# Attention head output copied whole, its halves crossed by transfers, a small add on another engine, and weight loads at other steps

## The chip, the core and the metric

The kernel runs on one core of one Trainium2 chip. The metric is the device time of one execution in microseconds (us), here the median of three timed runs. One further execution was profiled, and all rows below come from it. The engines are named as the profile names them: PE is TensorE (PEld is its weight load), DVE is VectorE, ACT is ScalarE, POOL is GpSimd, SP is SyncE, and SPq is the queue from which SP issues transfers.

## What is computed

Sixteen attention heads (batch 2, heads 8) over 768 rows of 64 values. A hash of six bits per row decides which keys a query may see. Two feed-forward layers follow, on 1536 tokens of 512 values with 2048 hidden values each.

```python
q_bucket = sum(((q @ proj) > 0) * 2 ** arange(6))          # the same for k
mask = q_bucket[..., :, None] == k_bucket[..., None, :]
scores = where(mask, (q @ k.T) / sqrt(64), -1e9)
scores = scores - max(scores)
attn = exp(scores)
attn = attn / (sum(attn) + 1e-09)
x = concat_heads(attn @ v)                                 # 1536 x 512
h = x @ moe_w_in;   x = (h * sigmoid(1.702 * h)) @ moe_w_out
h = x @ moe2_w_in;  out = (h * tanh(softplus(h))) @ moe2_w_out
```

## The kernel before, in words

Products are made in a rounded 32-bit form, and each operand is split into a high part and a low remainder, so that a product is two or three matmuls. The mask is a product too: each operand of the score product holds 32 rows of scaled bits (the mask rows) beside the remainder rows, and masked scores come out very large.

Attention is one loop over 96 steps, six for each head n (a step is one block of 128 queries against 768 keys). The source is written in the order in which each engine executes, and nothing is reordered. The letters of `ORDER = "ACaBbETQPR"` give the order within step i:

- A and B (`trp`): PE transposes two 128-key tiles of the three exponentiated blocks finished three steps earlier or less, and ACT copies each to its rounded high part (L421). a and b (`trl`): DVE subtracts to get the low part (L426).
- C (`clamp`): DVE clamps the scores and finds their minimum (L368). E (`expo`): ACT takes the exponential and sums each row into one column of `z` (L379).
- T: everything that was booked for this step by `at(step, function)`. Q (`qk`): the four score matmuls of the next step (L355), of which the last two read the mask rows.
- P and R (`pv`): four matmuls with the values (L438, L439). Three steps make one half (384 queries) of a head's weighted sum, in one PSUM tile `u`. After the sixth product of a half, `u_out` empties it.

Booked functions around the change, with step numbers for head n:

- `norm0` (L391, L392) at 6(n+1)+3: add 1e-9 to the row sums and take the reciprocal. `norm1` and `norm2` at 6(n+1)+5: transpose them on PE (L396), copy them out of PSUM (L402) and store them to DRAM (L403). `norm3` two steps later reads them back, broadcast to 64 partitions (`rb`, L409).
- `u_out` runs at the end of every third step, and for the second half of head n at 6(n+1)+3. Head pairs share tiles: `uh` takes each head's main half-sum at its own 64 partitions, `ul` takes the other 64 partitions crossed over. Both are ACT copies of 64x384 (L455, L456). The PSUM tile exists once, so the next half's first product waits for the second copy.
- `x_out` (POOL, L462, L463) adds `uh` and `ul` and multiplies by `rb`, at 12(u+1)+11 for pair u, and `x_split` (POOL) six steps later writes the tokens' high and low parts. For the last pair both run inside the feed-forward part.
- `start_prep` at 6(n-2)+2: POOL scales and splits q and k of head n (L251 to L258), with a transfer `qx<-qk_m` (L252). One head later, PE makes the hash bits (L266), DVE compares them (`mk`, L280), and at 6n-3 four transfers carry the mask rows to their operands (`qb<-mk`, `kb<-mk`, L292, L293). They are needed by the score matmuls of step 6n, which are issued at step 6n-1.
- Weights: `wfetch` starts 512 KB loads (`raw`, L103), three buffers in all. Five of them are converted inside attention (`wgo`: L112 and L126 on ACT, L114, L116, L118 on DVE, L128 on POOL), one in every second head from about step 31. Their loads are booked at st-15 and at st+6, where st is 32, 44, 56, 68 and 80.

All transfers are issued by SP in program order, and an issue that waits holds up those behind it. The feed-forward part `moe` follows; it issues one 12-matmul product after another on PE, while ACT and DVE convert weights, activate and split.

Of the kernel before, what the change touches and what calls it, by code (L numbers as in the profile page):

```python
# [10 lines left out]
F32 = mybir.dt.float32  # L11
# [3 lines left out]
ALU = mybir.AluOpType  # L15
# [21 lines left out]
def lsh_attention_moe_kernel(  # L37
# [10 lines left out]
    nc = tc.nc  # L48
    B, H, D, S = qt.shape
    NTOK, DM = out.shape  # L50
    P = 128
    NT = S // P
# [3 lines left out]
    HS = S // 2  # L56
# [4 lines left out]
    NPRE = 5  # L61
# [102 lines left out]
    def attention():  # L164
        with ExitStack() as es:
# [4 lines left out]
            sm = es.enter_context(tc.tile_pool(name="sm", bufs=12))  # L170
            ptp = es.enter_context(tc.tile_pool(name="ptp", bufs=4))
            uo = es_u.enter_context(tc.tile_pool(name="uo", bufs=2, side="right"))
# [168 lines left out]
            pt_t = {}  # L341
            u_t = {}
            xs_t = {}
            z_t = {}
            rb_t = {}
            scr = dr.tile([NHD, S], F32, name="scr")

            def qk(i):
                n, t = divmod(i, NT)
                kh, qx, qb, kb, _ = opnd[n]  # L350
                s = ps_s.tile([P, 2, 512], F32, tag="s", name="s")
                c = slice(t * P, (t + 1) * P)
                for a, bb, st in ((qx, kh, True), (qb, kb, False)):
                    for f in range(2):
                        nc.tensor.matmul(  # L355
                            s[:, f, :HS],
                            a[:, c],
                            bb[:, f * HS : (f + 1) * HS],
                            start=st,
                            stop=not st,  # L360
                        )
                st_t[i] = s
# [10 lines left out]
            def expo(i):  # L373
                sb, mn = st_t.pop(i)
                n, t = divmod(i, NT)
                p = sb.rearrange("p a b -> p (a b)")
                if t == 0:
                    z_t[n] = sm.tile([P, NT], F32, tag="z", name="z", bufs=2)
                nc.scalar.activation(  # L379
                    p,  # L380
                    p,
                    AF.Exp,
                    bias=mn,
                    scale=-1.0,
                    accum_out=z_t[n][:, t : t + 1],
                )
                p_t[i] = p

            def norm0(n):
                z = z_t[n]  # L390
                nc.vector.tensor_scalar(z, z, 1e-9, None, ALU.add)  # L391
                nc.vector.reciprocal(z, z)  # L392

            def norm1(n):
                pt = ps_t.tile([P, 512], F32, tag="pt", name="prep")
# [3 lines left out]
            def norm2(n):  # L399
                pt = z_t.pop(n)  # L400
                zt = sm.tile([NT, P], F32, tag="zt", name="zt", bufs=1)
                nc.vector.tensor_copy(zt, pt[:NT, :P])  # L402
                nc.sync.dma_start(scr[n].rearrange("(t p) -> t p", p=P), zt)  # L403

            def norm3(n):
# [25 lines left out]
            def pv(g, t):  # L431
                n, f = divmod(g, 2)
                hi, lo, _ = pt_t.pop((g, t))
                if t == 0:
                    u_t[g] = ps_u.tile([P, 512], F32, tag="u", name="u")
                ut = u_t[g]
                vv = opnd[n][4][0]
                nc.tensor.matmul(ut[:, :HS], vv[:, t, :], hi, start=(t == 0), stop=False)  # L438
                nc.tensor.matmul(ut[:, :HS], vv[:, t, :], lo, start=False, stop=(t == NT - 1))  # L439
                if t == NT - 1:  # L440
                    u_out(g)

            def u_out(g):
                n, f = divmod(g, 2)
                u, h = divmod(n, 2)
                ut = u_t.pop(g)
                if h == 0 and f == 0:
                    uh = uo.tile([P, S], F32, tag="uh", name="uh")
                    ul = uo.tile([P, S], F32, tag="ul", name="ul")
                    xs_t[u] = (uh, ul)  # L450
                uh, ul = xs_t[u]
                c = slice(f * HS, (f + 1) * HS)
                here = slice(h * D, (h + 1) * D)
                there = slice((1 - h) * D, (2 - h) * D)
                nc.scalar.copy(uh[here, c], ut[here, :HS])  # L455
                nc.scalar.copy(ul[here, c], ut[there, :HS])  # L456

            def x_out(u):
                uh, ul = xs_t.pop(u)
                rb = rb_t.pop(u)  # L460
                xs_t[u] = ul
                nc.gpsimd.tensor_add(ul, ul, uh)  # L462
                nc.gpsimd.tensor_mul(ul, ul, rb)  # L463

# [17 lines left out]
            second[2]()  # L482
            LAG = 3
            ORDER = "ACaBbETQPR"
            PVLAG = LAG + 1
            todo = {}

            def at(step, f, *args):
                todo.setdefault(step, []).append((f, args))

            def prep_at(n):
                return 5 if n == 2 else NT * (n - 2) + 2
# [14 lines left out]
            for u in range(NHD // 2 - 1):  # L507
                at(2 * NT * (u + 1) + XO, x_out, u)
                at(2 * NT * (u + 1) + XO + NT, x_split, u)
            for n in range(NHD):  # L510
                if n > 1:
                    at(prep_at(n), start_prep, n)
                if n >= 2:
                    at((0, 6)[n - 2] if n < 4 else NT * (n - 3) + 2, load_q, n)
                    at((0, 6)[n - 2] if n < 4 else NT * (n - 3) + 2, load_k, n)
                if n >= 2 and n % 2 == 0:
                    at(max(8, NT * (n - 2) + 1), load_v, n // 2)
                at(NT * (n + 1) + 3, norm0, n)
                at(NT * (n + 1) + 5, norm1, n)
                at(NT * (n + 1) + 5, norm2, n)  # L520
                at(NT * (n + 1) + 7, norm3, n)

            for k in range(NPRE):
                st = NSTEP - 4 - 2 * NT * (NPRE - k)
                at(st - 15, wfetch, k + 1)
                for off in (-1, 0, 2, 5, 8, 9):
                    at(st + off, wgo, k, 1, nc.gpsimd.tensor_sub)
                at(st + 6, wfetch, k + 4)
            at(NSTEP, load_table, SET_GELU)

            qk(0)
            for i in range(NSTEP + PVLAG):
                if i == NSTEP:
# [6 lines left out]
                g, j = divmod(kk, 3)  # L540
                kv = i - PVLAG
                gv, jv = divmod(kv, 3)
                for op in ORDER:
                    if op == "A" and tr:
                        trp(g, 2 * j)
                    elif op == "B" and tr:
                        trp(g, 2 * j + 1)
                    elif op == "a" and tr:
                        trl(g, 2 * j)
                    elif op == "b" and tr:  # L550
                        trl(g, 2 * j + 1)
                    elif op == "C" and i < NSTEP:
                        clamp(i)
                    elif op == "E" and i < NSTEP:
                        expo(i)
                    elif op == "Q" and i + 1 < NSTEP:
                        qk(i + 1)
                    elif op == "P" and 0 <= kv < NSTEP:
                        pv(gv, 2 * jv)
                    elif op == "R" and 0 <= kv < NSTEP:  # L560
                        pv(gv, 2 * jv + 1)
                    elif op == "T":
                        while todo and min(todo) <= i:
                            st = min(todo)
                            f, args = todo[st].pop(0)
                            if not todo[st]:
                                del todo[st]
                            f(*args)
                for part in range(max(0, 2 * (i - NSTEP)), min(2 * (i - NSTEP) + 2, 2 * KD)):
                    gemm_in(part // KD, part % KD, part % KD + 1)  # L570
            for st in sorted(todo):
                for f, args in todo[st]:
                    f(*args)
            late.append(lambda: x_out(NHD // 2 - 1))
            late.append(lambda: x_split(NHD // 2 - 1))

    def moe():
        with ExitStack() as es:
# [69 lines left out]
            for i in range(2, N + OLAG):  # L648
# [36 lines left out]
                gemm_out(i - OLAG)  # L685

    attention()
    moe()

# [56 lines left out]
```

## Time and profile before

| | us |
|---|---|
| median of three runs | 783.54 |
| lowest, highest | 782.67, 786.53 |
| the profiled execution | 783.52 |
| its span, first to last instruction | 781.5 |
| PE busy in the span | 758.0 |
| DVE, ACT, POOL busy | 434.6, 397.6, 184.4 |

The attention loop takes about the first 250 us and the two feed-forward layers the rest. [...] Busy time of PE is the union of pipelined matmuls with modelled ends, so a matmul that had to wait a little for its input still leaves a short tail that counts as busy.

### The profile page before, as it was taken

The page shows a single profiled execution, that of the slowest core. Times are in us where ns is not written, and L with a number is a line of the kernel's source. Part 1 is how long each engine was busy: PE and PEld are TensorE (multiplying, and loading weights), DVE is VectorE, ACT ScalarE, POOL GpSimd, SP SyncE. Part 2 cuts the span into 40 slices and gives each one's busy share as a digit, 9 for nine tenths or more (in the row PEclk, how much of TensorE's full clock was granted, in tenths as well). Part 3 has the DMA queues.
Part 4 walks back from the last instruction along what each step waited for, and adds up shares of the span by engine and source line. Part 5 has one row for each costly group of instructions (what it writes and reads, how often), then busy time and mean ns, then how long its engine had stood idle before and what let it go on. Part 6 is the DMA issues. An engine that isn't in the chain of part 4 may idle for free.

```text
span 781.5 us, 10532 instructions
## 1 busy us (share of the span) xinstructions
PE 758.0 (97%) x3760; PEld 642.4 (82%) x3760; DVE 434.6 (56%) x823; ACT 397.6 (51%) x796; POOL 184.4 (24%) x173
## 2 busy tenths in 40 slices
PE   5999999999999999999999999999999999999998
PEld 4999887888888788888888888888888888888886
DVE  6888889889897799941111677869311211121111
ACT  5888887888888466641212555466221212222121
POOL 7857867869633400000000000000000000000000
PEclk9999999999999999999999999999999999999999
DMA  5475574354420255610000144435000100010001
GB/s 164 131 177 129 134 201 133 88 150 122 114 74 20 68 202 199 201 69 1 0 1 1 64 152 162 135 96 174 0 1 1 54 1 1 0 55 1 0 1 54
DMA packets 23971, 65.04 MB, mean 83 GB/s; under 512 B 4048, under 2 KB 6192, under 8 KB 23920
## 3 DMA queue, kind: packets, MB, share of 16 engines
q1 hardware_dynamic: 23920, 64.39, 27.9%
q8 instruction: 29, 0.48, 0.3%
q14 instruction: 22, 0.18, 0.1%
HBM read 49.38 MB, written 3.19 MB: 67 GB/s over the span
## 4 chain that ended last, share of the span: by engine, by line
PE 79%; DVE 6%; ACT 5%; DMA 3%; POOL 3%; issue 3%; SPq 1%; DVEq 0%; POOLq 0%; ACTq 0%
PE y L612 33%; PE h L159 32%; PE s L355 4%; PE pt L414 4%; ACT p L379 2%; PE u L438 2%; PE u L439 2%; ACT pth L421 2%; PE prep L266 2%; POOL qx L254 1%; DMA vn<-in_vt_dram 1%; DMA kb<-mk 1%; DVE ptl L426 1%; DVE p L368 1%; DVE z L391 1%
## 5 line engine op out<-in xcount | busy, mean ns | idle before, releaser
L596 DVE TENSOR_TENSOR gl<-h,gh 128x512 fp32r<-128x512 f32 x96 | 66.2, 690 | 267.2 <-ACT h L595 266.8
L594 ACT ACTIVATE gh<-h 128x512 fp32r<-128x512 f32 x96 | 57.3, 597 | 256.1 <-PE h L159 255.5
L159 PE MATMUL h<-x_hi,wl 128*128 128x512 f32 x384 | 149.6, 389 | 0.9 <-DVE wl L128 0.9
L159 PE MATMUL h<-x_hi,wh 128*128 128x512 f32 x384 | 149.5, 389 | 0.0
L159 PE MATMUL h<-x_lo,wh 128*128 128x512 f32 x384 | 149.4, 389 | 0.0
L426 DVE TENSOR_TENSOR ptl<-pt,pth 128x384 fp32r<-128x384 f32 x192 | 97.8, 550 | 30.7 <-ACT pth L421 30.2
L379 ACT ACTIVATE p<-p,mn 128x768 f32<-128x768 f32 x96 | 90.5, 943 | 15.6 <-DVE p L368 15.1
L414 PE MATMUL pt<-ident,p 128*128 128x128 f32 x576 | 85.5, 277 | 8.8 <-DVE ptl L426 4.8
L421 ACT CAST pth<-pt 128x384 fp32r<-128x384 f32 x192 | 82.5, 483 | 22.1 <-PE pt L414 21.4
L368 DVE TENSOR_SCALAR_CACHE_REDUCE p<-s 128x768 f32<-128x768 f32 x96 | 90.2, 940 | 0.9 <-PE s L355 0.8
L159 PEld LDWEIGHTS h<-x_hi,wl 128*128 128x128 f32 x384 | 72.1, 188 | 16.3 <-DVE wl L128 1.3
L414 PEld LDWEIGHTS pt<-ident,p 128*128 128x128 f32 x576 | 66.7, 140 | 22.6 <-DVE ptl L426 9.8
L159 PEld LDWEIGHTS h<-x_hi,wh 128*128 128x128 f32 x384 | 72.1, 188 | 15.0 <-issue 0.2
L159 PEld LDWEIGHTS h<-x_lo,wh 128*128 128x128 f32 x384 | 72.0, 188 | 14.7
L612 PE MATMUL y<-gh,wl 128*128 128x512 f32 x192 | 74.8, 390 | 0.1
L612 PE MATMUL y<-gh,wh 128*128 128x512 f32 x192 | 74.7, 389 | 0.0
L612 PE MATMUL y<-wh,gh 128*128 128x512 f32 x192 | 74.7, 389 | 0.0
L612 PE MATMUL y<-wl,gh 128*128 128x512 f32 x192 | 74.7, 389 | 0.0
L612 PE MATMUL y<-gl,wh 128*128 128x512 f32 x192 | 74.7, 389 | 0.0
L612 PE MATMUL y<-wh,gl 128*128 128x512 f32 x192 | 74.7, 389 | 0.0
L438 PE MATMUL u<-pth,vv 128*128 128x384 f32 x192 | 65.8, 343 | 0.7 <-ACT ul L456 0.7
L439 PE MATMUL u<-ptl,vv 128*128 128x384 f32 x192 | 64.6, 337 | 0.0
(85 smaller groups left out, 1132.2 us busy)
## 6 DMA issues: line engine op xcount, KB each, us to landing
raw<-in_wt_dram SPq DMA_DIRECT2D x64, 512.0 KB, 3.3
kn<-in_kt_dram SPq DMA_DIRECT2D x16, 384.0 KB, 5.9
qn<-in_qt_dram SPq DMA_DIRECT2D x16, 192.0 KB, 4.2
vn<-in_vt_dram SPq DMA_DIRECT2D x8, 384.0 KB, 5.4
rb<-scr SPq DMA_DIRECT2D x16, 192.0 KB, 3.4
out_dram<-ob SPq DMA_DIRECT2D x12, 256.0 KB, 2.0
qx<-qk_m SPq DMA_DIRECT2D x15, 192.0 KB, 5.2
qb<-qk_m SPq DMA_DIRECT2D x15, 192.0 KB, 4.4
```

The source lines that it names most:

```text
L159: nc.tensor.matmul(h, a[:, wk], x[:, kk], start=(n == 0), stop=(n == 3 * KD - 1))
L355: nc.tensor.matmul(s[:, f, :HS], a[:, c], bb[:, f * HS : (f + 1) * HS], start=st, stop=not st,)
L368: nc.vector.tensor_scalar(sb, s[:, :, :HS], NEG, None, ALU.min, ALU.min, accum_out=mn)
L379: nc.scalar.activation(p, p, AF.Exp, bias=mn, scale=-1.0, accum_out=z_t[n][:, t : t + 1],)
L414: nc.tensor.transpose(ptile[:, j * P : (j + 1) * P], p_t[3 * g + j][:, t * P : (t + 1) * P], ident,)
L421: nc.scalar.copy(hi, ptile[:, :HS])
L426: nc.vector.tensor_sub(lo, ptile[:, :HS], rnd(hi))
L438: nc.tensor.matmul(ut[:, :HS], vv[:, t, :], hi, start=(t == 0), stop=False)
L439: nc.tensor.matmul(ut[:, :HS], vv[:, t, :], lo, start=False, stop=(t == NT - 1))
L594: nc.scalar.activation(gh, h, fn)
L596: nc.vector.tensor_sub(gl, h, rnd(gh))
L612: nc.tensor.matmul(y[j], w[:, js] if m == 0 else x[:, js], x if m == 0 else w, start=(first and n == 0), stop=(last and n == 2),)
```

## The change

`u_out` now makes one ACT copy of all 128 partitions of a half, into a tile for each head (`u0` for the first head of a pair, `u1` for the second). When a head is complete, SP transfers do the crossing: for the first head `ul[0:64] <- u0[64:128]`, for the second `ul[64:128] <- u1[0:64]` and `u0[64:128] <- u1[64:128]`, 192 KB each. The add of 1e-9 goes to POOL at step 6(n+1)+1 (the reciprocal stays on DVE at +3), the small copy of `norm2` goes from DVE to ACT, and the first five weight loads are booked at st-10 and three more at steps 76, 82 and 88.

```diff
             def norm0(n):
                 z = z_t[n]
-                nc.vector.tensor_scalar(z, z, 1e-9, None, ALU.add)
-                nc.vector.reciprocal(z, z)
+                nc.gpsimd.tensor_scalar(z, z, 1e-9, 1.0, ALU.add, ALU.mult)
+
+            def norm0b(n):
+                nc.vector.reciprocal(z_t[n], z_t[n])
...
-                nc.vector.tensor_copy(zt, pt[:NT, :P])
+                nc.scalar.copy(zt, pt[:NT, :P])
...
-                if h == 0 and f == 0:
-                    uh = uo.tile([P, S], F32, tag="uh", name="uh")
-                    ul = uo.tile([P, S], F32, tag="ul", name="ul")
-                    xs_t[u] = (uh, ul)
-                uh, ul = xs_t[u]
-                c = slice(f * HS, (f + 1) * HS)
-                here = slice(h * D, (h + 1) * D)
-                there = slice((1 - h) * D, (2 - h) * D)
-                nc.scalar.copy(uh[here, c], ut[here, :HS])
-                nc.scalar.copy(ul[here, c], ut[there, :HS])
+                if f == 0:
+                    uh_t[n] = uo.tile([P, S], F32, tag=f"u{h}", name="uh", bufs=2 - h)
+                uh = uh_t[n]
+                nc.scalar.copy(uh[:, f * HS : (f + 1) * HS], ut[:, :HS])
+                if f == 1 and h == 0:
+                    xs_t[u] = uo.tile([P, S], F32, tag="ul", name="ul")
+                    nc.sync.dma_start(xs_t[u][0:D], uh[D:P])
+                elif f == 1:
+                    nc.sync.dma_start(xs_t[u][D:P], uh[0:D])
+                    nc.sync.dma_start(uh_t[n - 1][D:P], uh[D:P])
...
+                at(NT * (n + 1) + 1, norm0, n)
+                at(NT * (n + 1) + 3, norm0b, n)
...
-                at(NT * (n + 1) + 3, norm0, n)
-                at(NT * (n + 1) + 5, norm1, n)
-                at(NT * (n + 1) + 5, norm2, n)
-                at(NT * (n + 1) + 7, norm3, n)
+                at(NT * (n + 1) + NZ, norm1, n)
+                at(NT * (n + 1) + NZ, norm2, n)
+                at(NT * (n + 1) + NZ + 2, norm3, n)
...
-                at(st - 15, wfetch, k + 1)
+                at(st - 10, wfetch, k + 1)
                 for off in (-1, 0, 2, 5, 8, 9):
                     at(st + off, wgo, k, 1, nc.gpsimd.tensor_sub)
-                at(st + 6, wfetch, k + 4)
+            for j in range(3):
+                at(st - 4 + 6 * j, wfetch, NPRE + 1 + j)
```

NZ is 5, so `norm1` to `norm3` keep their steps.

## Rows read from the trace of the kernel before

**Rows 1.** Windows: length, busy us (count) of each engine, clock, DMA share, GB/s.
```profile
35.00:91.60 56.60, 56.42 (x366) 52.41 (x365) 49.15 (x114) 50.08 (x115) 40.99 (x37) 1.00 0.60 145
91.60:232.30 140.70, 132.70 (x821) 116.60 (x821) 126.12 (x267) 117.49 (x262) 98.91 (x87) 1.00 0.47 126
...
281.50:330.00 48.50, 48.50 (x216) 40.17 (x215) 46.63 (x83) 32.45 (x56) 0.00 (x0) 1.00 0.61 200
```

**Rows 2.** Timeline, first score matmuls of chosen steps on PE: start, us, what.
```profile
35.04 0.60 PE L355 MATMUL s<-kh,qx 128*128 128x384 f32 x2
...
44.85 0.60 PE L355 MATMUL s<-kh,qx 128*128 128x384 f32 x2
46.92 0.59 PE L355 MATMUL s<-kh,qx 128*128 128x384 f32 x2
...
91.63 0.59 PE L355 MATMUL s<-kh,qx 128*128 128x384 f32 x2
...
119.57 0.60 PE L355 MATMUL s<-kh,qx 128*128 128x384 f32 x2
...
123.01 0.60 PE L355 MATMUL s<-kh,qx 128*128 128x384 f32 x2
...
232.32 0.60 PE L355 MATMUL s<-kh,qx 128*128 128x384 f32 x2
```

**Rows 3.** Groups by line on DVE, 91.6 to 232.3: busy us, mean ns, idle before.
```profile
L426 DVE TENSOR_TENSOR ptl<-pt,pth 128x384 fp32r<-128x384 f32 x108 | 55.0, 549 | 14.0 <-ACT pth L421 13.6
...
L391 DVE TENSOR_SCALAR z<-z 128x6 f32<-128x6 f32 x9 | 6.1, 677 | 0.0
...
L402 DVE COPY zt<-prep 6x128 f32<-6x128 f32 x9 | 2.4, 269 | 0.0
```

**Rows 4.** Timeline, DVE's small steps and POOL beside them.
```profile
104.21 0.15 DVE L391 TENSOR_SCALAR z<-z 128x6 f32<-128x6 f32 x1
...
150.74 1.83 POOL L463 TENSOR_TENSOR ul<-ul,rb 128x768 f32<-128x768 f32 x1
...
151.28 1.33 DVE L391 TENSOR_SCALAR z<-z 128x6 f32<-128x6 f32 x1
...
152.53 0.52 POOL L77 TENSOR_SCALAR vv<-vn 128x384 fp32r<-128x384 f32 x1
152.64 0.19 DVE L392 RECIPROCAL z<-z 128x6 f32<-128x6 f32 x1
```

**Rows 5.** Groups by line on ACT, the same stretch.
```profile
L456 ACT COPY ul<-u 64x384 f32<-64x384 f32 x18 | 8.5, 474 | 0.3
```

**Rows 6.** Waits in that stretch: us in total, times, longest.
```profile
POOL wl L128 <- ACT wh L126: 25.7, 4, 6.6
...
PEld s L355 <- DMA kb<-mk: 2.5, 5, 1.4
...
PE s L355 <- DMA kb<-mk: 1.3, 2, 1.1
```

**Rows 7.** Transfers: KB each, us to landing; stretches 58 to 60.7, 196.7 to 199.3, whole.
```profile
kb<-mk SPq DMA_DIRECT2D x2, 48.0 KB, 2.6
...
kb<-mk SPq DMA_DIRECT2D x2, 48.0 KB, 5.2
...
qx<-qk_m SPq DMA_DIRECT2D x15, 192.0 KB, 5.2
```

**Rows 8.** Timeline: the last mask-row transfer of a head, and PE waiting for it.
```profile
136.03 0.59 SPq L293 DMA_DIRECT2D kb<-mk  x1
...
139.35 0.19 PEld L355 LDWEIGHTS s<-kb,qb 128*128 128x128 f32 x1 [0.16 <-DMA kb<-mk]
```

**Rows 9.** Timeline of POOL and DVE where the feed-forward part begins.
```profile
258.91 1.85 POOL L462 TENSOR_TENSOR ul<-ul,uh 128x768 f32<-128x768 f32 x1 [14.44 <-ACT ul L456]
...
264.43 2.13 POOL L463 TENSOR_TENSOR ul<-ul,rb 128x768 f32<-128x768 f32 x1 [3.67 <-DMA rb<-scr]
...
264.77 2.33 DVE L128 TENSOR_TENSOR wl<-wb,wh 128x512 fp32r<-128x512 f32 x1
```

More of the change, by code (lines that the diff above doesn't have):

```diff
@@ L343, in attention @@
             xs_t = {}
+            uh_t = {}
             z_t = {}
@@ L377, in expo @@
                 if t == 0:
-                    z_t[n] = sm.tile([P, NT], F32, tag="z", name="z", bufs=2)
+                    z_t[n] = sm.tile([P, NT], F32, tag="z", name="z", bufs=3)
                 nc.scalar.activation(
@@ L446, in u_out @@
                 ut = u_t.pop(g)
-                if h == 0 and f == 0:
-                    uh = uo.tile([P, S], F32, tag="uh", name="uh")
-                    ul = uo.tile([P, S], F32, tag="ul", name="ul")
-                    xs_t[u] = (uh, ul)
-                uh, ul = xs_t[u]
-                c = slice(f * HS, (f + 1) * HS)
-                here = slice(h * D, (h + 1) * D)
-                there = slice((1 - h) * D, (2 - h) * D)
-                nc.scalar.copy(uh[here, c], ut[here, :HS])
-                nc.scalar.copy(ul[here, c], ut[there, :HS])
+                if f == 0:
[8 more added lines that the diff above has]
+                    nc.sync.dma_start(uh_t[n - 1][D:P], uh[D:P])
             def x_out(u):
-                uh, ul = xs_t.pop(u)
+                ul = xs_t[u]
+                uh = uh_t.pop(2 * u)
                 rb = rb_t.pop(u)
-                xs_t[u] = ul
                 nc.gpsimd.tensor_add(ul, ul, uh)
@@ L484, in attention @@
             ORDER = "ACaBbETQPR"
+            NZ = 5
             PVLAG = LAG + 1
```

## The prediction

> **What bounds the kernel now.** I read the windows first, then the starts of score matmuls, then the groups, waits and transfers of the stretch that stood out. The windows [rows 1] show three regimes. From 281.5 us PE is busy 48.50 of 48.50: the feed-forward part is PE's own work, the change doesn't touch it, and what attention gains moves all of it forward. From 35.0 to 91.6 (heads 2 to 5) PE is busy 56.42 of 56.60, and a head takes 56.59/4 = 14.15 us, from the starts at 35.04 and 91.63 [rows 2]. From 91.63 to 232.32 (heads 6 to 14, with the weight conversions) it is different: nine heads take 140.69 us, 15.63 each; PE is busy 132.7, DVE 126.1 of 140.7 (0.896) and ACT 117.5. A plain step lasts 46.92 - 44.85 = 2.07, but one such as 119.57 to 123.01 lasts 3.44 [rows 2]. No engine is full there; DVE is nearest to it for the work it has (PE's figure holds the tails of matmuls that waited), and its idle time, 14.0 us, waits for ACT's high parts [rows 3]. PE, DVE and ACT hand each other blocks in a ring, so what shortens DVE's or ACT's queue in these nine heads shortens the head.
>
> **Part 1, the add of 1e-9.** Alone, the DVE add takes 0.15 us. When POOL is inside a long operation it takes 1.33: it started at 151.28 and ended at 152.61, just as POOL's 1.83 us multiply (150.74 to 152.57) let go [rows 4]. There are four such adds in the stretch and five short ones, together 6.1 us [rows 3], so (6.1 - 5 x 0.15)/4 = 1.34 for a long one. Does the reciprocal, which stays, inherit the hold? It took 0.19 while POOL's next operation (152.53 to 153.05) ran [rows 4], so I cost that at nothing. [...]
>
> On POOL the add is a new 128x6 operation that no row shows. It is far smaller than the 128x384 one of 0.52 us [rows 4], so I bound it by 0 and 0.52 and take 0.2. It is covered: POOL is busy 98.9 of 140.7 [rows 1], and 25.7 us of its idle time are waits at the weight remainder alone [rows 6]. It also adds a wait. POOL's add stands at step 6(n+1)+1, ahead of the next preparation (L251 to L258), and must wait for the last exponential of head n. Behind it are that preparation, behind that in SP's queue the qx transfer, the q and k loads and then the mask rows. POOL now runs some steps ahead of the loop, so it loses lead, not time: what it prepares is used by PE six steps later. DVE's reciprocal in turn waits for POOL, with the next clamp behind it. Cost taken: 0; without that cover, up to 0.5 a head.
>
> **Part 2, the small copy to ACT.** DVE loses nine copies, 2.4 us [rows 3]. ACT gains nine, which I price at DVE's 0.27, between 0 and the 0.47 of a copy three times as long [rows 5]. It waits on PE's little transpose with the next high-part copy behind it. PE issues that transpose right after the transposes whose high parts ACT copies before its exponential, so it should be done. The store and the operand transfers behind it on SP come a little later, with steps to spare.
>
> **Part 3, one copy for two.** ACT loses 18 copies of 0.474 in the stretch, 8.5 us [rows 5], less the 9 x 0.27 = 2.4 of part 2: 6.1 net. The saving sits ahead of the high-part copy for which DVE waits, and the single `u` tile comes free 0.47 earlier. Outside the critical queue SP gets 24 transfers of 192 KB. Such a one between SBUF tiles lands in 5.2 us in the median (qx) [rows 7], and POOL's sum comes several steps later. What is queued behind them on SP: weight loads, the row-sum store, and operand transfers due six steps on. Cost taken inside attention: 0, from 0 to what the slower rival below gives.
>
> **Part 4, weight loads.** Mask rows land in 5.2 us in the median of a head with a load issued just ahead of them, against 2.6 in one without [rows 7]. PE waited 2.5 + 1.3 us for them in this stretch, partly the same time on two queues [rows 6]; moved loads should take most of this away.
>
> **The sum.** In the nine heads DVE's work falls from 126.1 by 6.1 + 2.4 to 117.6. If DVE stays as full as it is, 0.896, the stretch takes 131.2: a gain of 9.5. Parts 3 and 4 raise the share, for they shorten what DVE and PE wait for; I add 1.0 and take 10.5. The ends: only the hold itself, 4 x (1.33 - 0.15) = 4.7 [rows 4]; or all nine heads at the early pace, 140.7 - 9 x 14.15 = 13.3. In heads 2 to 5 PE has 0.2 us idle to give plus tails: 0.8 (0 to 2.0). Around head 15 one more long add: 0.5 (0 to 1.3).
>
> One cost: the last pair's sum runs while the feed-forward part begins. Now POOL adds at 258.91, when DVE has little to do, and its multiply at 264.43 stretches DVE's weight remainder to 2.33 us [rows 9]. After, the add must wait for transfers issued shortly before that time, which land up to 5.2 us later [rows 7], so some 1.9 us more of POOL work falls on DVE's weight conversion, to which PE is tied there: 1.0 (0 to 1.9). Sum: 10.5 + 0.8 + 0.5 - 1.0 = 10.8. Against the profiled 783.52 (span 781.5 and 2.0 around it; the median, 783.54, is the same) that is 772.7; I say 773.
>
> **The rivals.**
> *A. The mask rows take the place of the waits removed.* The chain from hash bits through `mk`, four issues of 0.6 us [rows 8] and the landing has a fixed length, while the steps beside it shrink. PE just waited (0.16) at 139.35 for the transfer issued at 136.03 [rows 8], so about 3.1 us from the last issue is all there is, against a landing of 2.6 without loads. For it: that margin is 0.5 us, and the long adds lie in this very window. Against it: in heads with a long add the margin is larger. It would leave some half of the sum: 10.8/2 = 5.4, 778 (775.5 to 781).
> *B. Slower: mask rows land behind the crossing transfers.* The 192 to 384 KB go out right after each head's mask rows, in all 15 heads, where weight loads were beside them in five. If landing rises from 2.6 midway to the loaded 5.2, to 3.9, PE waits 3.9 - 3.1 = 0.8 more a head, and at 5.2 it is 2.1: 15 x 0.8 to 2.1 = 12 to 32 us, against 10.8 gained, so 785 to 804, taken near the low end as 791. It decides where the landing passes 3.1 us plus what is gained per head (0.7). Against it: the loads that hurt were issued ahead, these go behind. [...] The trace shows only the case ahead (5.2), none behind.
> *C. The early pace.* All nine heads reach 14.15, with 2.0 and 1.3 beside it and no cost later: 783.5 - 13.3 - 2 to 3 = 768 or a little under.
> *D. No effect.* The ring is held by something not touched (PE's own order, the score product), and the shorter queues only lengthen other waits: 780 to 784. Against it: the 3.44 us steps coincide with the long adds.
>
> **How the numbers follow.** Forecast (770 to 777): 0.58. A: 0.20. B: 0.06. C: 0.08. D: 0.08. The range has to leave out about B, half of C and most of D: 767.5 to 780.5. A measurement of this kernel can tell about 0.5%, 3.9 us. Below 779.6 lie the forecast, C and 0.15 of A: 0.81. Within 0.5% lie the rest of A and D: 0.13. Slower: B, 0.06.
>
> **What would show it.** The nine heads from head 6 on take 128 to 132 us instead of 140.7; L391 is gone from DVE and its POOL form is near 0.2; the reciprocal stays at 0.19 without idle time before it; DVE's waits for high parts fall below 10 us; PE's waits for `kb<-mk` fall below 1.5. A reads as more waits of that kind, with a shorter landing; B as a landing above 3.8 us (3.1 + 0.7) in most heads; D as the same 15.6 us a head with less busy DVE. A POOL add that starts after DVE wants it would show as idle DVE ahead of the reciprocal, and would make me wrong in a way I hold unlikely. The weight remainder near the start of the feed-forward part should show one more long instance.

## The result, and the profile after

| | before | after |
|---|---|---|
| median, us | 783.31 | 773.87 |
| lowest to highest of four runs | 782.67 to 786.53 | 773.06 to 774.58 |
| ratio after/before, 95% interval | | 0.9862 (0.9833 to 0.9891) |
| profiled execution; its span | 783.52; 781.5 | 774.58; 772.7 |

The changed kernel is 1.4% faster: 9.4 us by the medians, 8.8 by the two spans (its profiled execution is the slowest of its four runs), against the 10.8 forecast. The windows say where. Columns as in [rows 1]; the limits are the starts of heads 2, 6 and 15, and in the last line the first matmul of the feed-forward part and the start of its seventh product, from which PE runs without a gap.

```profile
34.51:89.17 54.66, 54.66 (x368) 53.07 (x365) 48.39 (x106) 46.66 (x110) 41.53 (x40) 1.00 0.64 161
89.17:224.08 134.91, 126.01 (x823) 118.82 (x820) 124.64 (x249) 108.27 (x252) 100.29 (x98) 1.00 0.59 151
...
239.90:273.79 33.89, 31.85 (x147) 25.61 (x146) 25.44 (x39) 17.67 (x33) 10.45 (x9) 1.00 0.36 110
```

| stretch | before | after | gain | forecast |
|---|---|---|---|---|
| up to head 2 | 35.04 | 34.51 | 0.5 | 0 |
| heads 2 to 5 | 56.59 | 54.66 | 1.9 | 0.8 |
| heads 6 to 14 | 140.69 | 134.91 | 5.8 | 10.5 |
| head 15 to the end | 549.18 | 548.62 | 0.6 | 0.5 - 1.0 |

So the sum came out near the forecast, but its largest term was 4.7 us too large, and three small ones were too small by 2.7 together. The groups on DVE in heads 6 to 14 show what happened to the large one. First the weight conversion before (columns and stretch as in [rows 3]), then the lines after:

```profile
L118 DVE SCALAR_TENSOR_TENSOR wb<-wb,raw 128x512 uint32<-128x512 uint32 x5 | 5.4, 1079 | 0.0
...
L116 DVE SCALAR_TENSOR_TENSOR raw<-wb,raw 128x512 uint32<-128x512 uint32 x5 | 4.2, 843 | 0.0
L114 DVE TENSOR_SCALAR raw<-raw 128x512 uint32<-128x512 uint32 x4 | 3.5, 874 | 0.0
```

```profile
L429 DVE TENSOR_TENSOR ptl<-pt,pth 128x384 fp32r<-128x384 f32 x108 | 55.1, 551 | 8.7 <-ACT pth L424 8.7
...
L114 DVE TENSOR_SCALAR raw<-raw 128x512 uint32<-128x512 uint32 x4 | 8.1, 2030 | 0.0
L116 DVE SCALAR_TENSOR_TENSOR raw<-wb,raw 128x512 uint32<-128x512 uint32 x5 | 6.7, 1342 | 0.0
...
L118 DVE SCALAR_TENSOR_TENSOR wb<-wb,raw 128x512 uint32<-128x512 uint32 x5 | 4.1, 820 | 0.0
L395 DVE RECIPROCAL z<-z 128x6 f32<-128x6 f32 x9 | 1.6, 179 | 0.0
```

The long adds and the small copies are gone, and DVE waits 8.7 us for high parts where it waited 13.6 [rows 3]. But the three conversion steps (L114, the shift; L116, the merge; L118, the third), which the change doesn't touch, grew from 3.5 + 4.2 + 5.4 = 13.1 us to 8.1 + 6.7 + 4.1 = 18.9. The timeline shows the cause (start, us): before, a shift began in the middle of a POOL operation; after, one began 0.10 us into another and lasted until that was over.

```profile
146.81 1.86 POOL L258 TENSOR_TENSOR qk_m<-kn,kh 64x768 fp32r<-64x768 f32 x1
...
147.92 1.04 DVE L114 TENSOR_SCALAR raw<-raw 128x512 uint32<-128x512 uint32 x1
```

```profile
143.47 1.83 POOL L465 TENSOR_TENSOR ul<-ul,uh 128x768 f32<-128x768 f32 x1
143.57 2.02 DVE L114 TENSOR_SCALAR raw<-raw 128x512 uint32<-128x512 uint32 x1
```

It is the same kind of hold as on the add, which ended 0.04 us after POOL's operation [rows 4]: the shift of 1.04 us ends 0.29 after it, and so does the one of 2.02. The new add on POOL, and PE's waits for mask rows (columns as in [rows 6]):

```profile
L392 POOL TENSOR_SCALAR z<-z 128x6 f32<-128x6 f32 x9 | 1.8, 200 | 14.3 <-ACT p L380 14.0
```

```profile
PEld s L356 <- DMA kb<-mk: 2.4, 3, 1.8
...
PE s L356 <- DMA kb<-mk: 1.5, 1, 1.5
```

### The profile page after: what moved, and what is told of

The parts are those of the page before. It is cut to its first block, busy times and chain, and to the rows that moved or that the text cites. A ratio compares the mean times of both kernels' runs of the same rounds, so it can differ in the third digit from the quotient of the medians.

```text
span 772.7 us, 10578 instructions
## 1 busy us (share of the span) xinstructions
PE 748.9 (97%) x3760; PEld 645.5 (84%) x3760; DVE 431.8 (56%) x791; ACT 382.1 (49%) x780; POOL 186.4 (24%) x189
## 4 chain that ended last, share of the span: by engine, by line
PE 79%; POOL 6%; DVE 5%; issue 4%; DMA 3%; ACT 2%; SPq 1%; DVEq 0%; POOLq 0%; ACTq 0%
PE y L618 33%; PE h L159 33%; PE s L356 4%; PE pt L417 4%; PE u L442 2%; PE u L441 2%; DMA qn<-in_qt_dram 2%; DVE p L369 1%; PE prep L266 1%; ACT p L380 1%; DVE raw L116 1%; DVE ptl L429 1%; POOL qk_m L251 1%; POOL qk_m L258 1%; POOL qx L254 1%
## 5 line engine op out<-in xcount | busy, mean ns | idle before, releaser
L417 PE MATMUL pt<-ident,p 128*128 128x128 f32 x576 | 82.6, 274 | 8.9 <-DVE ptl L429 6.4
```

What stands on the lines that cost most here:

```text
L417: nc.tensor.transpose(ptile[:, j * P : (j + 1) * P], p_t[3 * g + j][:, t * P : (t + 1) * P], ident,)
```

## The experiments

The kernel before was timed again beside each group of runs, and the gains below are against its median there (784.03, 783.07 and 783.17). The changed kernel's gain is 9.4 us. Its ratio is known to 0.3%, so differences from it of some 2 us and less decide nothing by themselves; there the profile has to.

**Each part undone.** The add first:

```diff
-                nc.gpsimd.tensor_scalar(z, z, 1e-9, 1.0, ALU.add, ALU.mult)
+                pass
...
+                nc.vector.tensor_scalar(z_t[n], z_t[n], 1e-9, None, ALU.add)
                 nc.vector.reciprocal(z_t[n], z_t[n])
```

> The changed kernel with the add of 1e-9 back on VectorE, directly ahead of the reciprocal; the other three parts stay. Theory H (the add in GpSimd's queue waits for the exponentials, GpSimd loses its lead, and its long operations then meet VectorE's weight conversion): the conversion's first two steps fall from 2.03 and 1.34 us (mean, nine loaded heads) to about 1 us, but four long adds of 1.3 us come back, so the time stays at 773 to 775 us. Rival M (those holds come from the shorter steps, not from the add): they stay near 2 us, the long adds come on top, and the time is 777 to 779 us.

Measured 777.57, ratio 0.9918 (0.9900 to 0.9935): a gain of 6.5. The adds came back at 0.69 in the mean. The shift still took 1.63 and the merge 1.15, less than the 2.03 and 1.34 of the changed kernel, but not the 1 us of theory H:

```profile
L114 DVE TENSOR_SCALAR raw<-raw 128x512 uint32<-128x512 uint32 x4 | 6.5, 1630 | 0.0
L395 DVE TENSOR_SCALAR z<-z 128x6 f32<-128x6 f32 x9 | 6.2, 686 | 0.0
```

So the time is that of rival M, and the steps lie between the two forecasts. The cleaner test has no add at all:

```diff
-                nc.gpsimd.tensor_scalar(z, z, 1e-9, 1.0, ALU.add, ALU.mult)
+                pass
```

> The changed kernel with the add of 1e-9 left out altogether (each row sum is at least 1, so that the output does not change). Theory H: GpSimd keeps its lead, no add is held, the conversion's first step falls from 2.03 us to below 1.1 and the second from 1.34 to below 1.0; the time is 768 to 771 us. Rival M: the first step stays near 2 us and the time within 1 us of the changed kernel (773 to 774.5).

Measured 772.49, 0.9852 (0.9835 to 0.9868), a gain of 11.5. That lies between the two forecasts, but the profile decides against theory H: the shift (1.63) and the merge (1.43) are held without the add as well.

```profile
L116 DVE SCALAR_TENSOR_TENSOR raw<-wb,raw 128x512 uint32<-128x512 uint32 x5 | 7.2, 1430 | 0.0
L114 DVE TENSOR_SCALAR raw<-raw 128x512 uint32<-128x512 uint32 x4 | 6.5, 1634 | 0.0
```

So the add on POOL is not needed for these holds. Whether it costs anything itself is open: the gain without it is 2.1 us larger, at the edge of what can be told. Next, the copies of `u_out`:

```diff
-                nc.scalar.copy(uh[:, f * HS : (f + 1) * HS], ut[:, :HS])
+                nc.scalar.copy(uh[here, c], ut[here, :HS])
+                nc.scalar.copy(ul[here, c], ut[there, :HS])
...
```

> The changed kernel with the two ScalarE copies of 64 partitions for each half back, and no crossing transfers. Theory (the copy shortens the queue ahead of the high parts): heads 2 to 5 go back from 13.7 to about 14.1 us each and the whole takes 776 to 779 us. Rival B (the transfers cost something, by landing beside mask rows): the late mask rows of one head (1.8 us) vanish, and the time is 772 to 775 us.

Measured 780.80, 0.9956 (0.9942 to 0.9971): a gain of only 3.2, less than expected. Heads 2 to 4 took (77.30 - 34.91)/3 = 14.13 us each, as before the change; after it they took (75.55 - 34.51)/3 = 13.68. In heads 6 to 14 DVE waited 18.6 us for the high parts instead of 8.7:

```profile
L429 DVE TENSOR_TENSOR ptl<-pt,pth 128x384 fp32r<-128x384 f32 x108 | 55.0, 550 | 18.6 <-ACT pth L424 18.6
```

This is the largest part: 6.2 us go with it. The weight loads:

```diff
-                at(st - 10, wfetch, k + 1)
+                at(st - 15, wfetch, k + 1)
...
+                at(st + 6, wfetch, k + 4)
-            for j in range(3):
-                at(st - 4 + 6 * j, wfetch, NPRE + 1 + j)
```

> The changed kernel with the weight loads booked where they were. Theory (loads ahead of the mask rows delay them): TensorE waits more than 4 us for mask rows instead of about 2, and the time is 775 to 778 us. Rival (the one late landing left comes from the q and k loads or the crossing transfers, and the weight loads hardly matter with the rest of the change): 773 to 774.5 us.

Measured 776.83, 0.9912 (0.9893 to 0.9932): a gain of 7.2, 2.2 less than the changed kernel's. PE waited for mask rows 4.7 + 3.4 us, twice what it did before the change or after it:

```profile
PE s L356 <- DMA kb<-mk: 4.7, 4, 1.9
PEld s L356 <- DMA kb<-mk: 3.4, 5, 2.2
```

The waits are shown, their price is not. The execution profiled, at 774.92, is the fastest of six, and its nine heads took 134.70 us, as long as in the changed kernel (134.91): what the mask rows cost there, shorter holds gave back (the shift took 1.01 in the mean instead of 2.03).

And the small copy, back on DVE (`nc.vector.tensor_copy(zt, pt[:NT, :P])`):

> The changed kernel with the small copy of the reciprocals back on VectorE. Theory (VectorE is the fullest engine in nine heads, and nine copies of 0.2 us net come back): 774.5 to 776 us. Rival (it lies beside waits on either engine): 773 to 774.3 us.

Measured 773.33, 0.9871 (0.9854 to 0.9888), a gain of 9.8: the rival's time. Which engine makes the copy changes nothing that can be told.

**Parts alone, on the kernel before.** The single copy with its transfers:

> The kernel before with the single copy and the crossing transfers alone. Undoing this part cost 6.9 us. If the parts add up: 777 us. Theory (a ring: the long adds and the late mask rows hold the heads that the copy frees, so that alone it brings only what heads 2 to 5 gain, 1.9 us, and a part in the others): 779 to 781 us.

Measured 781.37, 0.9961 (0.9943 to 0.9979): 1.7 us, against the 9.4 - 3.2 = 6.2 that go when it is undone. Heads 2 to 5 have the gain in full (89.04 - 34.74 = 54.30 us). Heads 6 to 14 took 232.02 - 89.04 = 142.98 in the execution profiled (782.96, slower than the median), more than before: more waits for mask rows, and the merge held as in the changed kernel, the shift nearly so.

```profile
PE s L356 <- DMA kb<-mk: 3.3, 3, 1.5
PEld s L356 <- DMA kb<-mk: 3.2, 4, 1.9
```

```profile
L116 DVE SCALAR_TENSOR_TENSOR raw<-wb,raw 128x512 uint32<-128x512 uint32 x5 | 6.8, 1365 | 0.0
L114 DVE TENSOR_SCALAR raw<-raw 128x512 uint32<-128x512 uint32 x4 | 6.6, 1651 | 0.0
```

So the single copy alone, with the add still on DVE, moves the conversion onto POOL's long operations. The add on POOL alone (`norm0` at +1, reciprocal at +3, three `z` buffers):

> The kernel before with the add of 1e-9 alone moved to GpSimd, two steps earlier. If parts add up, 3.7 us less, as undoing it cost: 779 to 780 us. Theory (a hold that goes is replaced by holds on the conversion and by waits for mask rows): 781 to 783 us, with the conversion's first two steps above 1.2 us in the mean.

Measured 781.58, 0.9969 (0.9950 to 0.9987): 1.6 us, against 9.4 - 6.5 = 2.9 when undone. The time is the theory's; the reason given was only half right. The shift took 1.17 in the mean, the merge 0.88, no more than 0.84 before. Much of what DVE was given turned into waiting for ACT, whose two copies are still there; 17.3 us in heads 6 to 14, against 13.6 [rows 3]:

```profile
DVE ptl L428 <- ACT pth L423: 17.3, 28, 0.9
```

**Transfers doubled.** Does anything pay for the crossing? Every transfer is issued once more, into a tile that nobody reads:

```diff
                     nc.sync.dma_start(xs_t[u][0:D], uh[D:P])
+                    dup = uo.tile([P, S], F32, tag="dup", name="dup", bufs=1)
+                    uh_t["dup"] = dup
+                    nc.sync.dma_start(dup[0:D], uh[D:P])
...
```

> The changed kernel with every crossing transfer issued a second time, into a tile that nobody reads: 24 more transfers of 192 KB, right behind the first. Theory (transfers behind the mask rows cost nothing): 773 to 775 us. Rival B (they delay mask rows or what SP issues after them): over 777 us, with more than 6 us of TensorE waits for mask rows.

Measured 773.04, 0.9861 (0.9841 to 0.9882), a gain of 10.0. The one wait for `kb<-mk` left in heads 6 to 14:

```profile
PEld s L356 <- DMA kb<-mk: 0.4, 1, 0.4
```

Rival B of the prediction is out: what is issued behind the mask rows costs nothing that can be told here. In the same kernel the `kb<-mk` transfers landed in 2.9 us in the median, the doubled ones in 3.6.

**The price of the holds.** Two of DVE's conversion steps are booked where POOL waits: the shift ahead of the weight remainder, the merge ahead of the new add. The edit moves one thing more, which the expectation leaves out: ACT's first conversion step (L112), which stands ahead of the shift, goes from st-1 to st-5.

```diff
-                for off in (-1, 0, 2, 5, 8, 9):
+                for off in (-5, -4, 3, 5, 8, 9):
```

> The changed kernel with two of VectorE's weight-conversion steps booked elsewhere: the shift (L114) four steps earlier, into a stretch where GpSimd waits for the weight remainder, and the merge (L116) one step later, where GpSimd waits for the exponential. Nothing else changes. Theory P (what the nine loaded heads lack to the early pace is VectorE held by GpSimd's long operations): the two fall from 2.03 and 1.34 us to under 0.9 each, the nine heads from 134.9 to 126 to 129 us, the whole to 766 to 769 us. Rival (VectorE has slack there, the holds are hidden): shorter steps, but 773 to 774.5 us.

Measured 765.26, 0.9764 (0.9744 to 0.9785): 17.8 us less than before, and 8.4 more than the change gives. Heads 6 to 14 took 125.03 us, less than expected:

```profile
90.85:215.88 125.03, 123.84 (x822) 118.68 (x820) 114.70 (x249) 108.33 (x252) 100.63 (x98) 1.00 0.63 162
```

```profile
L116 DVE SCALAR_TENSOR_TENSOR raw<-wb,raw 128x512 uint32<-128x512 uint32 x5 | 3.5, 699 | 0.0
L114 DVE TENSOR_SCALAR raw<-raw 128x512 uint32<-128x512 uint32 x4 | 1.7, 420 | 0.0
```

DVE is busy 114.7 us where the changed kernel has 124.6, 9.9 less, and the stretch is shorter by as much, 134.91 - 125.03. Not all of that need be the holds: the changed kernel's execution has the late mask rows of one head (1.8 us, below), this one has none. As a bound, the same stretch with the three steps left out for the five blocks, and L112 where it was:

```diff
+        if k >= NPRE:
+            nc.vector.tensor_scalar(lw, lw, 29, None, ALU.logical_shift_right)
...
```

> The changed kernel without VectorE's three conversion steps for the five weight blocks that attention prepares (L114, L116, L118 are left out for them, so those weights stay unconverted; all waits around them, GpSimd's work and the loads stay). Theory P: the nine loaded heads run at the early pace of 13.65 us, 123 to 125 us in all, but for a late mask row or two; 762 to 765 us. Rival (transfers, mask rows or GpSimd's own work hold these heads): 768 us or more.

Measured 763.34, 0.9738 (0.9716 to 0.9761). Nine heads take 213.00 - 89.33 = 123.67, 13.74 each, from the starts:

```profile
89.33 0.60 PE L359 MATMUL s<-kh,qx 128*128 128x384 f32 x2
...
213.00 0.60 PE L359 MATMUL s<-kh,qx 128*128 128x384 f32 x2
```

So of the 11.2 us that the conversion still costs the changed kernel in these heads (134.91 - 123.67), 9.9 are gone in the kernel that keeps it clear of POOL, and 1.4 are left. The bound is reached without moving L112, so the gain doesn't hang on that. Does the gap for the merge come from the add's wait? The same move without the add:

> The kernel with the two conversion steps moved, and the add of 1e-9 left out besides (each row sum is at least 1). Theory W (the gap in which the merge step now runs exists because GpSimd waits there to add): without the add GpSimd fills the gap, the merge rises from 0.70 us to above 1.0 and the time from 765.3 to 767 to 770 us. Rival (the add only costs): 763 to 765 us.

Measured 772.55, 0.9855 (0.9836 to 0.9875): most of the move's gain is gone, more than theory W expected. The merge took 1.18 instead of 0.70; and the third step, which wasn't moved, lost more, 1.79 instead of 0.70, because it met a long operation of a POOL that runs ahead (L258; with the add POOL was two operations back, in L254, at 124.42):

```profile
L118 DVE SCALAR_TENSOR_TENSOR wb<-wb,raw 128x512 uint32<-128x512 uint32 x5 | 8.9, 1785 | 0.0
```

```profile
125.72 1.83 POOL L258 TENSOR_TENSOR qk_m<-kn,kh 64x768 fp32r<-64x768 f32 x1
125.89 2.21 DVE L118 SCALAR_TENSOR_TENSOR wb<-wb,raw 128x512 uint32<-128x512 uint32 x1
```

And the same move on the kernel before:

> The kernel before with the same two conversion steps moved and nothing else. Theory (before, VectorE is held mostly by the long adds and by ScalarE, and the two steps take 0.87 and 0.84 us there, so little is to be had): 781 to 783 us. Rival (it is the move alone that matters, with or without the change): 774 to 776 us, 8.6 us less as on the changed kernel.

Measured 780.01, 0.9953 (0.9938 to 0.9968): 3.2 us, a little more than expected and far from the 8.4. The reason given was not the right one: the move freed the adds too, which nobody had touched, 1.6 us in heads 6 to 14 instead of 6.1 [rows 3], so most of the holds were gone. DVE was busy 120.1 us instead of 126.1, but the nine heads (93.15 to 229.94) got only 3.9 us shorter, for DVE waited longer for ACT, whose two copies are still there: 15.9 us instead of 13.6.

```profile
L391 DVE TENSOR_SCALAR z<-z 128x6 f32<-128x6 f32 x9 | 1.6, 183 | 0.0
```

```profile
DVE ptl L426 <- ACT pth L421: 15.9, 22, 1.1
```

## Why the prediction was right, and where it was wrong

**The sum** was right in size, 10.8 for 8.8 by the spans, and in part by luck: its largest term was 4.7 us too large, more than twice the error of 2.0 that is left, and three small ones made up for the rest.

**Heads 6 to 14** were mis-sized, 10.5 for 5.8, and took 134.9 us, outside the 128 to 132 named as the sign. The step that failed is DVE's work, which was to fall from 126.1 to 117.6. Its share rose as forecast, and further: 10.5 means 117.6/130.2 = 0.903, and 124.64/134.91 = 0.924 was measured. The work fell to 124.6 only. Of the 7.0 missing, 5.8 are the conversion steps. I had read from [rows 4] that an operation of DVE can be held by POOL, taken one such operation off DVE, and left the others at their old lengths, although their means of 0.84 to 1.08, against 0.42 for the shortest shift (at 86.19) and 0.68 for the shortest merge and third step (at 91.46 and 193.69), said that they were held already. Here a hold depended on where two engines stood to each other: before, the same shift took 0.42 us at 86.19 and 1.04 at 147.92, and every other part of the change moved that. With the conversion out of POOL's way the term is 140.7 - 125.0 = 15.7 us. The other 1.2 us are covered by the 6.1 + 2.4 itself: records on DVE overlap their neighbours a little, and of the 8.5 us of adds and copies before, only 6.5 lie outside the other records of DVE, so its busy time could lose 2.0 less than was counted.

**Heads 2 to 5** gave 1.9 for 0.8. PE busy 56.42 of 56.60 [rows 1] read as if PE had nothing to give; but the same work kept it busy only 54.66 us after (x366 and x368 matmuls), so most of the 1.9 us lay in records counted as busy, by my estimate in the tails of matmuls that waited. It is the one copy that gave it: undone, the 14.1 us heads are back, alone, the gain is there in full.

**The add on POOL** took 0.200 for 0.2, with 14.0 us of waiting on POOL. The reciprocal had no idle time before it and took 0.179; it was never held (0.17 to 0.18 in all sixteen). Whether "it loses lead, not time" holds is open: without the add the gain is 2.1 us larger, at the edge of what can be told, and the late mask rows below are gone. In the best kernel it helps: with its wait the merge and the third step meet little of POOL's work and take 0.70 us each, 765.26; without the add both are held, 1.18 and 1.79, 772.55.

**The small copy** was put into DVE's work as a gain; it brought nothing that can be told.

**The mask rows.** Their waits did not fall below 1.5 us: 2.4 + 1.5, as much as before [rows 6], but nearly all in one head:

```profile
127.69 0.58 SPq L191 DMA_DIRECT2D kn<-in_kt_dram  x1
128.74 0.55 SPq L292 DMA_DIRECT2D qb<-mk  x1
...
130.60 0.59 SPq L293 DMA_DIRECT2D kb<-mk  x1
...
135.68 0.19 PEld L356 LDWEIGHTS s<-kb,qb 128*128 128x128 f32 x1 [1.81 <-DMA kb<-mk]
```

No weight load stands right ahead of it, but SP issued the load of k 1.05 us before the first mask row (127.69 to 128.74); in the other heads 6 to 14 with such a load it was 2.8 us or more. The same head in other runs falls roughly in order by this distance: PEld's longest wait for mask rows there was 0.61 us at 1.29 (`e1_no_conv_steps`), 0.70 at 1.39 (`u2_zt_on_dve`) and 0.58 at 1.73 (`t2_transfers_doubled`, for `qb<-mk`), and there was none at 2.17 (`n1_no_add`) and 2.19 (`s1_conv_moved`). So the load just ahead is the likely cause; no run moved it alone. Rival A was half true: with the old order of the weight loads the waiting doubles (4.7 + 3.4), but the 2.2 us that their move is worth by the medians are at the edge of what can be told. Rival B is shown wrong. Its price rested on one head: 5.2 [rows 7] was the slowest landing of the four loaded heads from 102 to 200 us; the other three had 4.2, 3.7 and 2.7.

**The start of the feed-forward part** cost what was said, but not where. The stretch from its first matmul to its seventh product took 33.89 us instead of 32.89, 1.0 more, as forecast; before it was

```profile
249.70:282.59 32.89, 31.76 (x147) 25.73 (x146) 24.55 (x41) 18.43 (x34) 8.13 (x6) 1.00 0.30 104
```

The one more long weight remainder, named as the sign, is not there. POOL's add at 251.85 held a third step instead (2.22 us), its multiply at 255.14 a merge (2.14): the mechanism forecast, on other steps. From the start of head 15 to the first feed-forward matmul the kernel gained 17.38 - 15.82 = 1.6 us, for 0.5.

## What to carry to other kernels

When a hold between two engines is seen on one instruction, look for it on all instructions of that kind, and compare their mean with their shortest: the excess is a sum that any shift of phase can raise or lower, here by 5.8 us of DVE's time one way and 9.9 the other, against a gain of 9.4 us for the whole change. In this ring of engines that are nearly equally full (PE, DVE and ACT busy 132.7, 126.1 and 117.5 of 140.7 us [rows 1]), parts did not add up (1.6 and 1.7 us alone, 2.9 and 6.2 when undone), so price a part at the kernel that it will stand in. Issue transfers that nobody waits for behind those that somebody does wait for: here the crossing, doubled behind the mask rows, cost nothing that can be told (773.04 against 773.87), and weight loads at their old place ahead of them went with 4.7 + 3.4 us of waits instead of 2.4 + 1.5.

## What the runs showed of the hardware

An operation of DVE that was held ended just after POOL's running one. Of those held in heads 6 to 14, before and after the change, the adds ended 0.02 to 0.04 us after it, the shifts 0.28 to 0.29, and the merges and third steps 0.53 to 0.55. An add of 0.15 us became 1.33 so, a shift of 0.42 became 2.02, a merge of 0.68 became 1.51 (at 118.21 in the changed kernel) and a third step of 0.68 became 2.21. The add and the shift have one SBUF input, the merge and the third step two: both kinds were held. Why these are held and others are not, no run shows.

POOL was held too. In the changed kernel its copy to `kh` took 1.35 us when a third step had started 0.02 us before it, against 0.82 at 110.95, and in the best kernel its add took up to 0.35 instead of 0.20 where it began 0.42 us into a merge. The earlier start did not decide in every case: in `b1_conv_moved_before` POOL's scaling of `qn` (L253) began at 125.45, 0.15 us ahead of a merge, and took 1.52 us instead of 0.83, while the merge took 0.67.

```profile
125.64 0.68 DVE L118 SCALAR_TENSOR_TENSOR wb<-wb,raw 128x512 uint32<-128x512 uint32 x1
125.66 1.35 POOL L77 TENSOR_SCALAR kh<-kn 128x768 fp32r<-128x768 f32 x1
```

The reciprocal, though it too goes from SBUF to SBUF and often ran beside a POOL operation, stayed at 0.17 to 0.19 us in every kernel. And ACT's copy out of PSUM took 0.474 us for 128 partitions, the same as for 64 [rows 5], which is why one copy for two halves that work:

```profile
L453 ACT COPY uh<-u 128x384 f32<-128x384 f32 x18 | 8.5, 474 | 0.0
```
